# Four weight and value loads joined in pairs, a longer whole part of the seventh w2, and a copy shared by two engines

## The chip, the cores and the metric

The kernel runs on one core of a Trainium2 chip. The metric is the device time of one execution in microseconds (us); the time before is the median of three runs, 179.95 us (179.82 to 180.35).

A core has five engines with an instruction queue each, which work in order: TensorE (PE), VectorE (DVE), ScalarE (ACT), GpSimd (POOL) and SyncE (SP). Data moves between the chip's memory and the on-chip memory by transfers that an engine issues and sixteen DMA engines carry out. In this kernel POOL issues the loads and SP the stores of the result.

## The reference

Attention over 8 batches of 8 heads with 576 rows of 64 values, then a mixture of 8 experts over 32 slots. Heads 0 to 3 see the last 32 positions ("plain"), heads 4 to 7 every fourth of the last 128 ("dilated"). Cut to what matters:

```python
scores = np.where(masks, (q @ k.T) / 8, -1e9)
attn = softmax(scores, axis=-1) @ v                 # 8 batches, 8 heads, 576 x 64
x = attn.transpose(0, 2, 1, 3).reshape(4608, 512)
logits = x @ phi                                    # phi: 512 x 32
slot_input = softmax(logits, axis=0).T @ x          # 32 slots x 512, four slots an expert
for e in range(8):                                  # w1: 512 x 1024, w2: 1024 x 512, each expert its own
    slot_out[4*e : 4*e+4] = np.maximum(slot_input[4*e : 4*e+4] @ w1[e], 0) @ w2[e]
out = softmax(logits, axis=1) @ slot_out            # 4608 x 512, float32
```

## The kernel before

Inputs are float32 in memory and are converted to float16 by the loads themselves; the output is float32.

**Homes.** On-chip memory for loads is four buffers (`home0`, `home2`, `home4`, `home6`) of 2 x 8192 float16 values in each of 128 partitions, so one half (`homes[b]`) for each of 8 batches. When batch b is done with, its half takes expert b's weights: w1 in its values 0 to 4095, w2 in 4096 to 8191.

**Loads.** All of them stand in POOL's queue in the order in which the code calls them. `load_batch(b)` (L180) issues for one batch: q and k of the plain heads, v (for batches from 2 on all eight heads in one load, L238), `vt` (the last 64 rows of v, L240), and q and k of the dilated heads, which batches 2/3, 4/5 and 6/7 share in one load for two batches (L207). The eight batches come first. The weights follow: w1 and w2 of experts 0/1 and 2/3 as pairs (`load_w1(e, 2)` L286, `load_both_w2` L293), issued in the loop over units after units 6 and 14; after unit 22 the pair w1(4,5) and the single w2(4); after unit 26 the single w1(6); behind the loop w1(7), w2(5), w2(6) and w2(7) (L732 to L735). A load waits until its place is free, that is until the engines have read the batch there, and until the load eight places ahead of it has landed: eight semaphores go round.

**The last two w2.** Each expert's w2 lies as 8 chunks of 512 columns. The seventh one, w2(6), comes in three loads: chunks 0 to HALF-1 whole (HALF = 4, L309), then the other chunks' columns 0 to 255 (side 0) and 256 to 511 (side 1) by `load_half` (L300). The eighth, w2(7), comes by sides, each in two pieces of 6 and 2 chunks (L325). The order is: w2(6) whole part, w2(6) side 0, w2(7) side 0, w2(6) side 1, w2(7) side 1. So side 0 of the slots' output can be finished while side 1 is still being loaded.

**Compute.** The loop runs over 32 units (a batch and a pair of heads). Behind it comes a part whose order on PE, DVE and ACT is written out by hand (from L737). In it the experts run in pairs `pr`: `expert_in(pr)` (L794) multiplies the slots with both w1, `expert_turn(pr)` (L809) transposes the result (DVE copies it, L818), `expert_out(e)` (L823) multiplies with w2 and adds into one accumulator `sop`. PE's order (L837 to L848) is

```python
    expert_in(0)
    expert_in(1)
    for pr in range(4):
        expert_turn(pr)
        if pr < 2:
            expert_in(pr + 2)
        if pr == 1:
            front_sums(B - 1, ring.tile([128, 11, N_SLOTS], FP32, name="sums", tag="ring"))
        if pr < 3:
            expert_out(2 * pr)
            expert_out(2 * pr + 1)
    expert_out(6, chs=range(HALF))
```

Then, for each side (L892), come the rest of `expert_out(6)`, `expert_out(7)`, a copy of that side of `sop` to float16 (`so`, L895: side 0 by ACT, side 1 by DVE), and for the first three of nine output tiles of 512 rows four finishing matmuls each (`f`, L865), whose results ACT and DVE scale in turn into `ot` (L869, L871), and a store by SP (L881). The other six tiles are finished over the whole width at the end (L887).

In the texts below out(e) is `expert_out(e)`, in(pr) is `expert_in(pr)`, and w1(6,7) is one load for two experts.

Of the kernel before, what the change touches and what calls it, by code (L numbers as in the profile page):

```python
# [14 lines left out]
H = 8  # L15
S = 576
D = 64
# [6 lines left out]
E_EXP = 8  # L24
# [6 lines left out]
RP, NP = 6, 96  # L31
RD = 24
# [5 lines left out]
NV = 2  # L38
SIDES = ((0, DMODEL // 2), (DMODEL // 2, DMODEL))
PIECES = ((0, 6), (6, 8))  # L40
HALF = 4
FIRST_TILES = 3
PAIRED = (2, 4, 6)
TOGETHER = ((3,), (4, 5), (6,), (7,), (8,))
# [3 lines left out]
def kernel(  # L48
# [10 lines left out]
    nc = tc.nc  # L59
# [13 lines left out]
    first = {}  # L73
    for n, (nm, ten, by) in enumerate((("qp", q, nc.sync), ("kp", k, nc.scalar))):
        first[nm] = stage[0:NP, 768 * n : 768 * n + 768].rearrange("p (g x) -> p g x", g=2)
        by.dma_start(
            out=first[nm],
            in_=ten[0, 0:2].rearrange("h s d -> (h s) d").rearrange("(g p r) d -> p g (r d)", g=2, r=RP),
# [8 lines left out]
    for n in (1, 2, 4, 8, 16, 32, 64, 128):  # L87
        m = min(n, QW - n)
        nc.vector.tensor_scalar(
            out=count[:, n : n + m], in0=count[:, 0:m], scalar1=float(n), scalar2=None, op0=ALU.add  # L90
# [28 lines left out]
    vp = [kept([128, NKB + 1, 4, D + 1], f"vp{i}") for i in range(NV)]  # L119
    vd = [kept([128, 16, D + 1], f"vd{i}") for i in range(2)]  # L120
# [18 lines left out]
    twos = [big.tile([128, 2, 8192], FP16, name=f"home{i}", tag=f"home{i}") for i in (0, 2, 4)]  # L139
# [40 lines left out]
    def load_batch(b):  # L180
        if b == 6:
            twos.append(big.tile([128, 2, 8192], FP16, name="home6", tag="home6"))
            homes.extend(twos[3][:, i] for i in range(2))
        t = homes[b]
        parts = raws.setdefault(b, {})
        at = 0

        def load_v(nm, h0, n_h, r0, dst):
            n_p = dst.shape[0]
            dst = dst.rearrange("p (h x) -> p h x", h=n_h)  # L190
            nc.gpsimd.dma_start(  # L191
                out=dst,
                in_=v[b, h0 : h0 + n_h, r0 : r0 + 4 * n_p, :].rearrange(
                    "h (p r) d -> p h (r d)", r=4
                ),
            )
            parts[nm] = dst.rearrange("p h (r d) -> p h r d", r=4)

        for nm, ten, hs, rows in (
            ("qp", q, 0, RP), ("kp", k, 0, RP), ("qd", q, 4, RD), ("kd", k, 4, RD),  # L200
        ):
            g = 4 * S // (NP * rows)
            n = g * rows * D
            if nm in ("qd", "kd") and b & 6 in PAIRED:
                if b % 2 == 0:
                    both = twos[b // 2][0:NP, :, at : at + n]
                    nc.gpsimd.dma_start(  # L207
                        out=both,
                        in_=ten[b : b + 2, hs : hs + 4].rearrange("e h s d -> e (h s) d").rearrange(
                            "e (p r) d -> p e (r d)", r=rows  # L210
                        ),
                    )
                    for i in range(2):
                        raws.setdefault(b + i, {})[nm] = both[:, i : i + 1]
                at += n
                continue
            parts[nm] = t[0:NP, at : at + n].rearrange("p (g x) -> p g x", g=g)
            at += n
            src = ten[b, hs : hs + 4].rearrange("h s d -> (h s) d").rearrange(
                "(g p r) d -> p g (r d)", g=g, r=rows  # L220
            )
            if b == 0 and nm in first:
                t0 = side_by_side(nm[0], 0)
                nc.vector.tensor_copy(
                    out=t0.rearrange("p r (h d) -> p r h d", h=2),
                    in_=first[nm].rearrange("p h (r d) -> p r h d", d=D),
                )
                nc.gpsimd.dma_start(out=parts[nm][:, 2:4], in_=src[:, 2:4])
            else:
                nc.gpsimd.dma_start(out=parts[nm], in_=src)  # L230
            if nm == "kp":
                if b == 0:
                    head_v = t[:, 6144:7168].rearrange("p (h x) -> p h x", h=4)
                    parts["vp"] = head_v.rearrange("p h (r d) -> p h r d", r=4)
                elif b < 2:
                    load_v("vp", 0, 4, 0, t[:, 6144:7168])
                else:
                    load_v("v", 0, 8, 0, t[:, 6144:8192])  # L238
                    parts["vp"], parts["vd"] = parts["v"][:, 0:4], parts["v"][:, 4:8]
                load_v("vt", 0, 8, 512, t[96:112, 0:2048])  # L240
        if b < 2:
            load_v("vd", 4, 4, 0, t[:, 7168:8192])

    def cast_first_v():
# [35 lines left out]
    def load_w1(e, n=1):  # L280
        for i in range(e, e + n):
            w_tiles[i] = [
                homes[i][:, 0:4096].rearrange("p (c f) -> p c f", c=4),
                homes[i][:, 4096:8192].rearrange("p (c f) -> p c f", c=8),
            ]
        nc.gpsimd.dma_start(  # L286
            out=homes[e][:, 0:4096] if n == 1 else twos[e // 2][:, :, 0:4096],
            in_=moe_w1[e].rearrange("(p c) f -> p (c f)", p=128) if n == 1
            else moe_w1[e : e + 2].rearrange("e (p c) f -> p e (c f)", p=128),
        )  # L290

    def load_both_w2(e):
        nc.gpsimd.dma_start(  # L293
            out=twos[e // 2][:, :, 4096:8192],
            in_=moe_w2[e : e + 2].rearrange("e (p c) f -> p e (c f)", p=128),
        )
# [8 lines left out]
    def load_w2(e):  # L305
        w2t = w_tiles[e][1]
        w2_from = moe_w2[e].rearrange("(p c) f -> p c f", p=128)
        if e == E_EXP - 2:
            nc.gpsimd.dma_start(  # L309
                out=w2t[:, 0:HALF].rearrange("p c f -> p (c f)"),  # L310
                in_=w2_from[:, 0:HALF].rearrange("p c f -> p (c f)"),
            )
            load_half(e, 0)
            return
        if e < E_EXP - 2:
            nc.gpsimd.dma_start(
                out=w2t.rearrange("p c f -> p (c f)"), in_=w2_from.rearrange("p c f -> p (c f)")
            )
            return
        w2t = w_tiles[e][1] = w2t.rearrange("p c f -> p (c f)").rearrange("p (s c f) -> p s c f", s=2, c=8)  # L320
        for n, (d0, d1) in enumerate(SIDES):
            if n == 1:
                load_half(e - 1, 1)
            for c0, c1 in PIECES:
                nc.gpsimd.dma_start(out=w2t[:, n, c0:c1], in_=w2_from[:, c0:c1, d0:d1])  # L325
# [350 lines left out]
    for u in range(NU - 2):  # L676
        b, ph = divmod(u, 4)
        if ph == 0:
            st = scores(u + 1)
            softmax_parts(u + 1, st)  # L680
            if u:
                x_transposes(u - 1)
            values(u)
        elif ph == 1:
            st = scores(u + 1)
            if b + 1 < B:
                regroup(4 * b + 4)
            if b:
                front_logits(b - 1)
            if b + 1 < B:  # L690
                transposes(4 * b + 4)
            values(u)
            x_transposes(u - 1)
            softmax_parts(u + 1, st)
        elif ph == 2:
            st = scores(u + 1)
            values(u)
            if b + 1 < B:
                regroup(4 * b + 6)
            softmax_parts(u + 1, st)  # L700
            if b + 1 < B:
                dilated_transposes(b + 1, "k")
                dilated_transposes(b + 1, "q")
            if b:
                front_rows(b - 1)
            x_transposes(u - 1)
            if u == 2:
                nc.vector.tensor_copy(out=vd[1][:, 0, 0:1], in_=xs[0][:, 0, 2 * D : 2 * D + 1])
        else:
            st = scores(u + 1)  # L710
            if b:
                front_slots(b - 1)
            values(u)
            softmax_parts(u + 1, st)
            if b + 1 < B:
                select_v(b + 1)
                transposes(4 * b + 6)
            x_transposes(u - 1)
            if b + 1 < B:
                spread_v(b + 1)  # L720
        if u in (6, 14):
            load_w1(u // 4 - 1, 2)
            load_both_w2(u // 4 - 1)
        if u == 22:
            load_w1(4, 2)
            load_w2(4)
        if u == 26:
            load_w1(6)
        if 26 <= u:
            nc.gpsimd.memset(hTp[u - 26], 0.0)  # L730

    load_w1(E_EXP - 1)  # L732
    load_w2(E_EXP - 3)
    load_w2(E_EXP - 2)
    load_w2(E_EXP - 1)  # L735

# [25 lines left out]
    for c in range(2):  # L762
# [14 lines left out]
        out=siT,  # L777
# [114 lines left out]
    for n, (d0, d1) in enumerate(SIDES):  # L892
        expert_out(E_EXP - 2, n, range(HALF, 8))
        expert_out(E_EXP - 1, n)
        (nc.scalar.copy if n == 0 else nc.vector.tensor_copy)(out=so[:, d0:d1], in_=sop[:, d0:d1])  # L895
        for i in range(FIRST_TILES):
            finish_half(i, n)
    for tiles in TOGETHER:
# [35 lines left out]
```

## Time and profile before

| what | value |
|---|---|
| median of three runs | 179.95 us (179.82 to 180.35) |
| the profiled execution, its time | 180.08 us |
| its span, first to last instruction | 177.9 us |
| PE, ACT, DVE, POOL busy | 82%, 70%, 68%, 24% of the span |
| moved by DMA | 41.28 MB in 27094 packets |
| read from and written to the chip's memory | 61.93 MB and 9.44 MB, 401 GB/s over the span |
| first store of the result issued at | 152.15 us |
| last store of the result issued | in a row of five that starts at 160.25 us and lasts 6.92 us |

Times inside the execution count from the span's start. The profile's page divides the span into 40 equal slices; each digit of a row is the busy share of a slice in tenths, the row DMA is the mean over the sixteen DMA engines, and the row GB/s says what they moved. The bytes of a converting load are counted as float16, half of what is read. A stretch's line gives its length, then for each engine the busy us and the number of instructions, then the granted clock of TensorE as a share of the full one, the DMA share and GB/s. A timeline's line gives start, duration, engine, line, operation, result and operands, and in brackets how long the engine had been idle and what ended that. The DMA share can be above 1 where packets of one engine overlap.

### The profile page before, as it was taken

The numbers are of one execution on the slowest core, as the hardware profiler recorded it, in microseconds if no ns is written. First come the engines' busy times: TensorE is split into PE (matmuls) and PEld (weight loads), VectorE is DVE, ScalarE is ACT, GpSimd is POOL, SyncE is SP. The second block draws the span as 40 slices with busy tenths as digits, with TensorE's granted clock in tenths as the row PEclk, the third lists the DMA queues.
The fourth block names the chain that finished last, engine by engine and source line by source line (L and its number), as shares of the span: only waits on it lengthen the run. The fifth ranks groups of instructions, "written<-read, shape, count | busy, mean of one in ns | idle before, by whom it ended". The sixth has DMA issues, their size and how long they took to land.

```text
span 177.9 us, 5105 instructions
## 1 busy us (share of the span) xinstructions
PE 145.3 (82%) x2137; PEld 99.4 (56%) x2137; DVE 120.3 (68%) x337; ACT 124.0 (70%) x233; POOL 43.2 (24%) x68
## 2 busy tenths in 40 slices
PE   6589889899999999999999999977899833897200
PEld 2367576687676676776677676755763311453000
DVE  7959896987988888898798898587120100689400
ACT  2588899999998998998998999952304100699300
POOL 7756443334333441001000500700011100000000
PEclk9987999999999999999999999996558985569955
DMA  5999999999999999999999999999999999999996
GB/s 162 243 198 207 199 205 212 199 200 204 212 200 201 202 213 199 217 223 214 214 219 215 215 217 217 214 219 214 214 221 214 208 197 194 252 382 423 431 424 267
DMA packets 27094, 41.28 MB, mean 232 GB/s; under 512 B 1344, under 2 KB 22848, under 8 KB 24512
## 3 DMA queue, kind: packets, MB, share of 16 engines
q0 software_dynamic: 22080, 30.41, 96.1%
q1 hardware_dynamic: 4784, 10.26, 14.9%
q10 hardware_dynamic: 208, 0.29, 0.6%
q8 instruction: 16, 0.26, 0.5%
q14 instruction: 6, 0.05, 0.1%
HBM read 61.93 MB, written 9.44 MB: 401 GB/s over the span
## 4 chain that ended last, share of the span: by engine, by line
DMA 47%; PE 31%; ACT 6%; DVE 5%; issue 2%; POOL 1%; DVEq 0%; ACTq 0%; POOLq 0%
DMA home<-in_moe_w_dram 37%; DMA home<-in_k_dram 9%; PE o L496 6%; PE f L865 4%; PE s L391 3%; PE rgx L516 3%; PE sel L270 2%; PE sel L259 2%; ACT kTd L364 2%; PE rgq L351 2%; ACT pd L424 2%; PE rgk L351 2%; PE l L534 1%; DVE ot L871 1%; ACT ot L869 1%
## 5 line engine op out<-in xcount | busy, mean ns | idle before, releaser
L501 DVE TENSOR_TENSOR x<-o,rc 128x640 f16<-128x640 f32 x32 | 26.6, 831 | 0.2
L417 ACT ACTIVATE pr<-s 128x960 f16<-128x960 f32 (+1 forms) x32 | 25.2, 795 | 0.0
L424 ACT ACTIVATE pd<-s 128x640 f16<-128x640 f32 x32 | 22.3, 719 | 1.1 <-PE s L400 1.0
L871 DVE TENSOR_SCALAR ot<-f,rrow 128x256 f32<-128x256 f32 (+1 forms) x24 | 13.2, 613 | 7.8 <-PE f L865 7.8
L433 DVE TENSOR_TENSOR Pp<-pr,fixed 128x1280 f16<-128x1280 f16 (+1 forms) x32 | 15.4, 520 | 0.0
L496 PE MATMUL o<-vd,P 128*128 128x65 f16 x256 | 15.1, 197 | 0.2 <-DVE x L501 0.2
L191 POOL DMA_DIRECT2D home<-in_v_dram x17 | 12.0, 709 | 13.1 <-DMA home<-in_k_dram 6.1
L869 ACT ACTIVATE ot<-f,rrow 128x256 f32<-128x256 f32 (+1 forms) x24 | 12.7, 583 | 2.6 <-PE f L865 2.2
L496 PE MATMUL o<-vp,Pp 128*128 128x65 f16 x288 | 13.7, 197 | 1.0 <-DVE x L501 1.0
L516 PE MATMUL rgx<-fixed,x 128*128 128x128 f16 x155 | 14.0, 222 | 0.6 <-ACT qTd L364 0.4
L865 PE MATMUL f<-so,ET 128*128 128x256 f16 (+1 forms) x48 | 12.3, 411 | 2.2 <-ACT ot L869 1.1
L286 POOL DMA_DIRECT2D home<-in_moe_w_dram x5 | 3.2, 637 | 41.5 <-PE sel L270 38.0
L352 ACT COPY qT<-rgq 128x576 f16<-128x576 f16 x16 | 10.3, 645 | 4.0 <-PE rgq L351 3.9
L391 PE MATMUL s<-qT,kTp 64*128 64x160 f16 (+1 forms) x160 | 10.6, 224 | 2.9 <-ACT pd L424 1.9
L534 PE MATMUL l<-xT,phi 128*128 128x288 f16 x64 | 11.6, 307 | 1.6 <-DVE xT L526 1.6
L496 PEld LDWEIGHTS <-P 128*128 128x128 f16 x288 | 11.8, 99 | 1.8 <-DVE xT L526 0.2
L522 ACT COPY xT<-rgx 128x512 f16<-128x512 f16 x16 | 9.7, 605 | 4.3 <-PE rgx L516 4.3
L496 PEld LDWEIGHTS <-Pp 128*128 128x128 f16 x288 | 11.1, 99 | 2.4 <-DVE x L501 1.2
L363 PEld LDWEIGHTS <-home 96*128 96x128 f16 x192 | 10.5, 100 | 3.1 <-DMA home<-in_k_dram 1.0
L391 PE MATMUL s<-qTd,kTd 64*128 64x144 f16 x128 | 12.1, 230 | 0.0
L443 DVE TENSOR_TENSOR P<-pd,fixed 128x1024 f16<-128x1024 f16 x16 | 10.9, 681 | 1.8 <-ACT pd L424 1.8
L516 PEld LDWEIGHTS <-x 128*128 128x128 f16 x160 | 10.2, 98 | 3.1 <-DVE x L501 1.6
(136 smaller groups left out, 318.3 us busy)
## 6 DMA issues: line engine op xcount, KB each, us to landing
home<-in_moe_w_dram POOLq DMA_DIRECT2D x5, 2048.0 KB, 38.9
home<-in_moe_w_dram POOLq DMA_DIRECT2D x4, 1024.0 KB, 33.9
out_dram<-ot SPq DMA_DIRECT2D x4, 1024.0 KB, 8.5
home<-in_v_dram POOLq DMA_DIRECT2D x6, 512.0 KB, 14.3
home<-in_q_dram POOLq DMA_DIRECT2D x9, 288.0 KB, 12.9
home<-in_k_dram POOLq DMA_DIRECT2D x9, 288.0 KB, 13.4
out_dram<-ot SPq DMA_DIRECT2D x4, 512.0 KB, 3.6
out_dram<-ot SPq DMA_DIRECT2D x1, 2048.0 KB, 6.8
```

What stands on the lines that cost most here:

```text
L191: nc.gpsimd.dma_start(out=dst, in_=v[b, h0 : h0 + n_h, r0 : r0 + 4 * n_p, :].rearrange("h (p r) d -> p h (r d)", r=4),)
L391: nc.tensor.matmul(st[:, g, at : at + n], kT[64 * g : 64 * g + 64, k0 : k0 + 128], qT[64 * g : 64 * g + 64, q0 : q0 + n], start=True, stop ...
L417: nc.scalar.activation(out=(pr[:, :, 0 : 3 * QW], pr[:, :, 3 * QW :])[part], in_=st[:, :, 0 : (480, 224)[part]], func=AF.Exp, scale=SCALE,)
L424: nc.scalar.activation(out=pr[:, part].rearrange("p c e t -> p e c t"), in_=st[:, :, 0 : 2 * DW].rearrange("p e (c t) -> p e c t", c=2), f ...
L433: nc.vector.tensor_tensor(out=Pp[:, :, b0 : b0 + nb, 0:w], in0=pr[:, :, b0 * QW : b0 * QW + nb * w].rearrange("p h (t c) -> p h t c", c=w) ...
L496: nc.tensor.matmul(ot[:, h, blk], lhs, rhs, start=(n == 0), stop=(n == len(mms) - 1), skip_group_check=True)
L501: nc.vector.tensor_tensor(out=xs[b][:, :, 2 * D * hp : 2 * D * hp + 2 * D].rearrange("p t (h d) -> p h t d", h=2), in0=ot[:, :, :, 0:D], i ...
L516: nc.tensor.transpose(rg[:, 128 * blk : 128 * blk + 128], x[:, blk, hl : hl + 128], ident)
L534: nc.tensor.matmul(lp, phi4[:, kc].rearrange("p a s -> p (a s)"), xT[:, kc, 288 * c : 288 * c + 288], start=(kc == 0), stop=(kc == 3), ski ...
L865: nc.tensor.matmul(fp, ET[:, c0 : c0 + 127 * nj + 1 : nj], so[:, d0:d1], start=True, stop=True)
L869: nc.scalar.activation(out=ot[:, j], in_=fp, func=AF.Copy, scale=scale)
L871: nc.vector.tensor_scalar(out=ot[:, j], in0=fp, scalar1=scale, scalar2=None, op0=ALU.mult)
```

## The change

- v of batches 4 and 5 comes in one load, and v of batches 6 and 7 too. Batches 2 and 3 keep their own. For this q, k and v of the paired batches get other places in the home, and in the paired batches v is issued ahead of the dilated q and k as before.
- w2(4) and w2(5) come as a pair after unit 22, where w2(4) alone was issued. w1(6) and w1(7) come as a pair behind the loop; w1(6) after unit 26 is gone. So w2(5) goes ahead of w1(6) and w1(7) in POOL's queue.
- HALF is 6: six chunks of w2(6) come whole, and two by sides. `expert_out(6)` ahead of the sides takes six chunks.
- The copy of each side of `sop` is split by columns, 128 by ACT and 128 by DVE.

The diff, cut to its core:

```diff
-HALF = 4
+HALF = 6
...
         def load_v(nm, h0, n_h, r0, dst):
...
+                in_=v.rearrange("b h s d -> (b h) s d")[
+                    H * b + h0 : H * b + h0 + n_h, r0 : r0 + 4 * n_p, :
+                ].rearrange("h (p r) d -> p h (r d)", r=4),
...
+        at = (10240 + 2 * n * (b % 2)) if paired else 0
...
+        if paired:
+            if b < 4:
+                load_v("v", 0, H, 0, t[:, 6144:8192] if b == 2 else t[:, 0:2048])
+            elif b % 2 == 0:
+                load_v("v", 0, 2 * H, 0, flat[:, 6144:10240])
+            load_v("vt", 0, H, 512, t[96:112, 2048:4096])
+            parts["vp"], parts["vd"] = parts["v"][:, 0:4], parts["v"][:, 4:8]
...
         if u == 22:
             load_w1(4, 2)
-            load_w2(4)
-        if u == 26:
-            load_w1(6)
+            load_both_w2(4)
...
-    load_w1(E_EXP - 1)
-    load_w2(E_EXP - 3)
+    load_w1(E_EXP - 2, 2)
     load_w2(E_EXP - 2)
     load_w2(E_EXP - 1)
...
-        (nc.scalar.copy if n == 0 else nc.vector.tensor_copy)(out=so[:, d0:d1], in_=sop[:, d0:d1])
+        mid = (d0 + d1) // 2
+        nc.scalar.copy(out=so[:, d0:mid], in_=sop[:, d0:mid])
+        nc.vector.tensor_copy(out=so[:, mid:d1], in_=sop[:, mid:d1])
```

More of the change, by code (lines that the diff above doesn't have):

```diff
@@ L185, in load_batch @@
         parts = raws.setdefault(b, {})
-        at = 0
+        paired = b & 6 in PAIRED
+        flat = twos[b // 2].rearrange("p e x -> p (e x)")
+        n = S * 4 * D // NP
         def load_v(nm, h0, n_h, r0, dst):
@@ L192, in load_v @@
                 out=dst,
-                in_=v[b, h0 : h0 + n_h, r0 : r0 + 4 * n_p, :].rearrange(
-                    "h (p r) d -> p h (r d)", r=4
-                ),
-            )
[L197 to L217, printed above, removed]
+                in_=v.rearrange("b h s d -> (b h) s d")[
+                    H * b + h0 : H * b + h0 + n_h, r0 : r0 + 4 * n_p, :
+                ].rearrange("h (p r) d -> p h (r d)", r=4),
+            )
+            got = dst.rearrange("p h (r d) -> p h r d", r=4)
+            if n_h <= H:
+                parts[nm] = got
+            else:
+                for i in range(2):
+                    raws.setdefault(b + i, {})[nm] = got[:, H * i : H * i + H]
+        at = (10240 + 2 * n * (b % 2)) if paired else 0
+        for nm, ten in (("qp", q), ("kp", k)):
+            home = flat if paired else t
+            parts[nm] = home[0:NP, at : at + n].rearrange("p (g x) -> p g x", g=4)
             at += n
[L219 to L222, printed above, removed]
+            src = ten[b, 0:4].rearrange("h s d -> (h s) d").rearrange("(g p r) d -> p g (r d)", g=4, r=RP)
+            if b == 0:
                 t0 = side_by_side(nm[0], 0)
@@ L230, in load_batch @@
                 nc.gpsimd.dma_start(out=parts[nm], in_=src)
[L231 to L241, printed above, removed]
+        if b == 0:
+            head_v = t[:, 6144:7168].rearrange("p (h x) -> p h x", h=4)
+            parts["vp"] = head_v.rearrange("p h (r d) -> p h r d", r=4)
+        elif not paired:
+            load_v("vp", 0, 4, 0, t[:, 6144:7168])
+        if paired:
[5 more added lines that the diff above has]
+            parts["vp"], parts["vd"] = parts["v"][:, 0:4], parts["v"][:, 4:8]
+        else:
+            load_v("vt", 0, H, 512, t[96:112, 0:2048])
+        for i, (nm, ten) in enumerate((("qd", q), ("kd", k))):
+            if not paired:
+                at = 3072 + n * i
+                parts[nm] = t[0:NP, at : at + n][:, None, :]
+                nc.gpsimd.dma_start(
+                    out=t[0:NP, at : at + n],
+                    in_=ten[b, 4:8].rearrange("h s d -> (h s) d").rearrange("(p r) d -> p (r d)", r=RD),
+                )
+            elif b % 2 == 0:
+                both = flat[0:NP, 2 * n * i : 2 * n * i + 2 * n].rearrange("p (e x) -> p e x", e=2)
+                nc.gpsimd.dma_start(
+                    out=both,
+                    in_=ten[b : b + 2, 4:8].rearrange("e h s d -> e (h s) d").rearrange(
+                        "e (p r) d -> p e (r d)", r=RD
+                    ),
+                )
+                for j in range(2):
+                    raws.setdefault(b + j, {})[nm] = both[:, j : j + 1]
+        if not paired:
             load_v("vd", 4, 4, 0, t[:, 7168:8192])
```

## The prediction

> **What bounds the kernel now.** I read the page's slices first, then the chain of waits, then stretches of the last 55 us, then PE's timeline there.
>
> ```profile
> DMA  5999999999999999999999999999999999999996
> GB/s 162 243 198 207 199 205 212 199 200 204 212 200 201 202 213 199 217 223 214 214 219 215 215 217 217 214 219 214 214 221 214 208 197 194 252 382 423 431 424 267
> ```
>
> The DMA row is full from the second slice to the last but one. Loads convert f32 to f16, so 215 GB/s counted at the f16 side is about 430 GB/s read, the rate at which the f32 outputs leave (423 to 431). The core is bound by its 16 DMA engines nearly throughout; the attention work of PE, ACT and DVE lies beside it. The next answer gives, for each stretch, its length, busy us of each engine, the granted clock, the DMA share and GB/s.
>
> ```profile
> 74.49:124.00 49.51, 45.38 (x797) 33.78 (x795) 41.26 (x104) 42.42 (x82) 7.22 (x12) 0.97 1.03 216
> 124.00:144.00 20.00, 17.07 (x204) 10.13 (x204) 3.19 (x15) 3.87 (x9) 3.00 (x4) 0.73 1.03 213
> 144.00:151.00 7.00, 2.67 (x29) 0.96 (x22) 0.26 (x2) 0.37 (x1) 0.00 (x0) 0.59 1.40 196
> 151.00:153.50 2.50, 2.50 (x12) 1.57 (x11) 1.93 (x5) 2.14 (x6) 0.00 (x0) 0.50 0.95 150
> 153.50:162.00 8.50, 7.33 (x38) 3.72 (x38) 6.96 (x14) 6.64 (x15) 0.00 (x0) 0.68 1.08 386
> 162.00:176.00 14.00, 3.30 (x11) 1.13 (x10) 4.77 (x8) 3.93 (x7) 0.00 (x0) 0.75 1.01 428
> ```
>
> One stretch is not full: 150 GB/s at 151.0 to 153.5. The trace marks a load's completion once per DMA engine, and the marks of the very last load spread from 151.25 to 154.11: seven engines are done by 152.1, nine only after 153.1. So the end has two bounds. The slowest engine: loads done at 154.11, plus the outputs (3.15 MB at 386 GB/s, 8.15 us, and 6.29 MB at 428, 14.7 us) gives 176.96; the last output lands at 177.00. The fast engines wait for outputs: the first is issued at 152.15, they have written it at 154.10 and the last one at 176.59, 24.44 us after that first issue. The slack between the two bounds is only 0.4 us. What the change does to **the last load** and to **the first output's issue** decides.
>
> The first output hangs on side 0 of the slots, as PE's timeline shows (start, duration, what, and in brackets idle time and what ended it).
>
> ```profile
> 137.85 0.40 PE L799 MATMUL h<-home,siT 128*32 128x512 f16 x2
> 138.76 1.08 PE L799 MATMUL h<-home,siT 128*32 128x512 f16 x14 [0.50 <-DMA home<-in_moe_w_dram]
> 139.77 0.43 PE L584 MATMUL sums<-quarter,ET 128*128 128x1 f16 x8
> 140.13 1.05 PE L828 MATMUL sop<-home,hTp 128*32 128x512 f16 x16
> 141.10 0.41 PE L813 MATMUL tp<-fixed,hs 128*128 128x128 f16 x4
> 141.79 0.62 PE L828 MATMUL sop<-home,hTp 128*32 128x512 f16 x8 [0.27 <-DVE hTp L818]
> 143.63 0.62 PE L828 MATMUL sop<-home,hTp 128*32 128x512 f16 x8 [1.22 <-DMA home<-in_moe_w_dram]
> 144.18 0.41 PE L813 MATMUL tp<-fixed,hs 128*128 128x128 f16 x4
> 146.14 0.62 PE L828 MATMUL sop<-home,hTp 128*32 128x512 f16 x4 [1.55 <-DMA home<-in_moe_w_dram]
> 147.46 0.41 PE L828 MATMUL sop<-home,hTp 128*32 128x256 f16 x4 [0.71 <-DMA home<-in_moe_w_dram]
> 149.41 1.07 PE L828 MATMUL sop<-home,hTp 128*32 128x256 f16 x8 [1.54 <-DMA home<-in_moe_w_dram]
> ```
>
> The starts behind a DMA date the landings: seventh w1 pair's second half 138.7, sixth w2 143.6, then 2.51 us for 512 KB whole, 1.32 for 256 KB in half rows, 1.95 for 384 KB; the last 128 KB (0.68) lands at 150.05.
>
> **Four loads fewer.** Pairs of w1(6,7), w2(4,5), v(4,5) and v(6,7) replace eight loads by four; bytes and run lengths stay. What does one load cost beside its bytes? On the engine that marks first, half-row loads take 0.675 us for 128 KB, 1.33 for 256, 2.00 for 384: a straight line with 0.01 us at zero. Two single 1 MB loads take 4.85 and 4.87, a 2 MB pair 9.71: 0.01. The short v tails of 64 KB take 0.35 to 0.46 where the bytes are worth 0.33: up to 0.13, part of it their row shape. A loss is excluded on the queue, since POOL issues 15 to 39 us before landing and six to eight loads wait at any time. Bounds 0 to 0.13 each; I take 0.025, nearest to the rows of the same sizes: 4 x 0.025 = **-0.1 us**. The 0.5 to 0.9 us of POOL per issue lie under that queue.
>
> [...]
>
> The v pairs put 512 KB (2.7 us) ahead of the rest of batches 4 and 6. Batch 4's kd lands at 50.9 and its transposes begin at 64: covered by 10 us.
>
> **Six chunks whole.** 256 KB change from half rows (1.32) to whole rows (2.51 / 2 = 1.25): **-0.07**. Loads thus end at 154.11 - 0.17 = 153.94. But side 0 now waits for more: 768 KB whole (3.77) + 0.68 + 1.95 + 0.68 = 7.08 us behind the sixth w2, instead of 2.51 + 1.32 + 1.95 + 0.68 = 6.46. With the -0.1, its last piece lands at 150.05 + 0.62 - 0.1 = **150.57**.
>
> **The moved w1.** w2(5) goes ahead of w1(7), and w1(6,7) has one completion: both land where w2(5) did, near 143.5 instead of 133.9 and 138.7. PE executes in order, and behind expert_in(3) are queued the sums, out(2) to out(5), two turns and out(6): all that ran from 137.85 to 146.7 now starts at 143.5. Its length, wave by wave (four matmuls side by side): at full clock in(3) 0.9, sums 0.46, out(2,3) 0.86, turn with DVE's copy 0.78, out(4,5) 0.86, turn 0.78, out(6) six chunks 0.43, side 0's last ten matmuls and drain 0.58: 5.65 us. At half clock a wave takes 0.427 instead of 0.216 (rows at 132 to 134), and the same list gives 10.0.
>
> Which clock? In stretches of 2 us the granted clock is 0.50 until 135.0, 1.00 until 145.2, 0.50 until 158.9: it rose after a full 3.4 us of matmuls, and fell after 3.4 us with PE 45% busy. PE would now idle from 137.9 to 143.5, 5.6 us, so I take half clock at the start and a rise at the end of the first full window, 148.6 if the windows fall as here. Then 5.1 of 10.0 are done by 148.6 and the rest takes 4.9 x 0.565 = 2.8: side 0 is complete at **151.4**, against 150.49. PE, not the load (150.57 + 0.3), is late next. By the window's phase the rise lies between 146.6 and 150.0: 150.9 (the load's bound) to 152.0.
>
> [...]
>
> **The slots' copy.** ScalarE took 0.37 for 256 columns and 0.60 for 512, so 0.26 for 128; VectorE 0.42 for 256 and 0.21 for 64, so 0.28. The longer of two beside each other: 0.28 against 0.37, -0.09 on side 0. Side 1's 0.42 - 0.28 lies under outputs already queued: 0. The risk that the second engine is busy is nil on side 0 (both idle since 144.9). At full clock the first two finishing matmuls end some 0.2 earlier (second starts 0.11 instead of 0.21 later, drain 0.1 shorter): -0.2.
>
> **Sum.** First output: 152.15 + 0.91 - 0.09 - 0.2 = 152.77, so 24.44 later the engines end at 177.21; the slowest engine's own bound is 177.00 - 0.17 = 176.83. The later counts: +0.2 us. The profiled execution took 180.08 (span 177.93), 0.13 above the median of 179.95. So 179.95 + 0.2 = **180.1** (180.15 cut to tenths). Own range, by 0.1 either way in the loads and by a rise at 146.6 to 149: 179.7 to 180.5.
>
> **Rivals.**
> Slower, one mechanism: PE's clock comes back late. Each us of rise beyond 148.6 costs 0.43. At 150.0, side 0 is complete at 152.0 and the end is 180.7; if the clock stays at half, 153.5, the 0.2 is gone too, and the end is 182.4. It decides from a rise at 149.5. For it: 62% and 83% busy windows at 148.6 to 155.5 did not raise it, and the new stretch has gaps at the two turns. Against: without waits for DMA these gaps are some 0.3 us. Chance 0.25.
> Faster: the loads are cheaper by the upper bound (4 x 0.13, 0.5 us) and the clock rises early, so that the load bounds side 0 at 150.2 + 0.3: first output 152.15 + 0.0 - 0.29 = 151.9, and the slowest engine ends at 177.00 - 0.6: 179.35. For it: the short v tails. Against: the sizes that are really paired show 0.01. Chance 0.18.
> [...] The equal spacing of queued loads leaves it 0.02. That the change does less than it says is excluded: in the built programs POOL issues 56 loads instead of 60, and PE's order changes only where out(6) takes six chunks.
>
> **Numbers.** Forecast 0.55, slower rival 0.25, faster 0.2. 0.3%, 0.54 us, is about what a measurement of this kernel can tell from no change. The range takes in the faster rival and the slower one up to a rise 2.4 us late (0.43 x 2.4 = 1.0): 179.3 to 181.2.
>
> **What would show it.** Right: PE idle from about 138 until the pair lands near 143.5, a granted clock of 0.5 there and 1.0 before 149; side 0's copy near 151.4; the first output at 152.8; the 150 GB/s stretch emptier and later; the last load at 153.9. Wrong: a pair of w1 that lands before 142 (loads cost more than I took), a clock that did not fall in PE's idle time, or outputs that do not keep their 24.44 us.

## The result, and the profile after

The changed kernel takes 180.48 us (median of 22 runs), the kernel before 179.84 (22 runs beside them). The ratio is 1.0041, 95% interval 1.0023 to 1.0059: slower by 0.2 to 0.6%. More telling than the median is the spread. The kernel before lies between 179.71 and 180.36. The changed one begins at the same place, 179.79, and reaches 181.55: fifteen of its 22 runs lie between 179.79 and 180.95, the other seven between 181.42 and 181.55.

The profiled execution is the fastest of them, 179.79 us with a span of 177.9. So it shows the change at its best, and the long runs have to be read from the experiments. The rows of its page that answer to those of before:

```profile
DMA  5999999999999999999999999999999999999996
GB/s 149 247 199 206 199 202 214 200 199 200 208 211 198 199 209 207 221 215 219 212 217 219 214 217 217 214 215 221 214 212 223 211 199 194 231 385 422 433 425 282
```

The DMA row is as full as before. The same stretches (length, busy us of each engine, granted clock, DMA share, GB/s) show the change at the end:

```profile
144.00:151.00 7.00, 6.28 (x80) 2.46 (x69) 0.72 (x5) 0.69 (x2) 0.00 (x0) 0.77 1.32 194
151.00:153.50 2.50, 1.93 (x15) 1.23 (x15) 1.82 (x5) 1.82 (x6) 0.00 (x0) 1.00 0.85 116
153.50:162.00 8.50, 6.96 (x40) 3.67 (x40) 7.83 (x17) 7.57 (x17) 0.00 (x0) 1.00 1.08 385
```

PE is busy for 6.28 us from 144 to 151, where it had 2.67. The stretch that was not full moves 116 GB/s instead of 150: the DMA engines that are done with their loads wait longer, since the first store is issued at 152.55 instead of 152.15. PE's timeline says why it is busy so late:

```profile
139.82 0.41 PE L822 MATMUL tp<-fixed,hs 128*128 128x128 f16 x4
143.58 1.72 PE L808 MATMUL h<-home,siT 128*32 128x512 f16 x16 [3.34 <-DMA home<-in_moe_w_dram]
145.24 0.42 PE L596 MATMUL sums<-quarter,ET 128*128 128x1 f16 x8
145.59 1.84 PE L837 MATMUL sop<-home,hTp 128*32 128x512 f16 x16
147.36 0.41 PE L822 MATMUL tp<-fixed,hs 128*128 128x128 f16 x4
148.04 1.05 PE L837 MATMUL sop<-home,hTp 128*32 128x512 f16 x16 [0.27 <-DVE hTp L827]
149.02 0.41 PE L822 MATMUL tp<-fixed,hs 128*128 128x128 f16 x4
149.70 1.18 PE L837 MATMUL sop<-home,hTp 128*32 128x512 f16 x16 [0.27 <-DVE hTp L827]
151.55 0.71 PE L874 MATMUL f<-so,ET 128*128 128x256 f16 x5 [0.68 <-DVE so L906]
```

The second line is in(3): it waited until w1(6,7) landed. Sixteen of `sop`'s matmuls take 1.84 us at 145.6 and 1.05 at 148.0: the granted clock was 0.50 from 143.8 to 147.2 and 1.00 behind it. Here the list ends with side 0's last load (150.55), so the late w1 costs nothing in this run. The copies and the first store, in the timelines of ACT, DVE and SP:

```profile
150.91 0.27 ACT L905 CAST so<-sop 128x128 f16<-128x128 f32 x1 [4.91 <-PE sop L837]
```
```profile
151.21 0.29 DVE L906 CAST so<-sop 128x128 f16<-128x128 f32 x1 [1.48 <-ACT so L905]
```
```profile
152.55 5.87 SPq L890 DMA_DIRECT2D out_dram<-ot  x8
```

The two half copies do not run beside each other: DVE's waits for ACT's and starts 0.03 us after its end.

### The profile page after: what moved, and what is told of

Its sections match the earlier page's. It is cut to its first block, busy times and chain, and to the rows that moved or that the text cites. A ratio compares the mean times of both kernels' runs of the same rounds, so it can differ in the third digit from the quotient of the medians.

```text
span 177.9 us, 5100 instructions
## 1 busy us (share of the span) xinstructions
PE 145.7 (82%) x2135; PEld 99.9 (56%) x2135; DVE 120.4 (68%) x338; ACT 123.5 (69%) x234; POOL 40.4 (23%) x64
## 4 chain that ended last, share of the span: by engine, by line
PE 49%; DVE 13%; ACT 12%; DMA 11%; issue 7%; POOL 0%; DVEq 0%; ACTq 0%; POOLq 0%
DMA home<-in_moe_w_dram 11%; PE o L508 11%; PE s L403 5%; PE rgx L528 4%; PE sel L282 4%; PE sel L271 4%; ACT ot L878 4%; ACT kTd L376 3%; DVE P L455 3%; PE warm L480 3%; PE rgq L363 3%; PE rgk L363 2%; ACT pd L436 2%; PE l L546 2%; PE u L609 2%
## 5 line engine op out<-in xcount | busy, mean ns | idle before, releaser
L878 ACT ACTIVATE ot<-f,rrow 128x256 f32<-128x256 f32 (+1 forms) x24 | 11.9, 604 | 1.7 <-DMA home<-in_moe_w_dram 0.7
L874 PE MATMUL f<-so,ET 128*128 128x256 f16 (+1 forms) x48 | 10.7, 324 | 2.5 <-DVE so L906 1.4
L193 POOL DMA_DIRECT2D home<-in_v_dram x15 | 10.8, 717 | 8.4 <-DMA home<-in_q_dram 3.9
```

What stands on the lines that cost most here:

```text
L193: nc.gpsimd.dma_start(out=dst, in_=v.rearrange("b h s d -> (b h) s d")[H * b + h0 : H * b + h0 + n_h, r0 : r0 + 4 * n_p, :].rearrange("h ( ...
L878: nc.scalar.activation(out=ot[:, j], in_=fp, func=AF.Copy, scale=scale)
```

## The experiments

Two theories stood. The first: **PE's list behind the late w1** ends last, at a clock that differs from run to run, and the copy and the later load of side 0 add to it. The second: the **joined loads** themselves, or the six whole chunks, cost the time. Eleven kernels were run beside the kernel before.

| kernel | runs | median, lowest to highest, us | ratio to before (interval) | first store issued, us |
|---|---|---|---|---|
| the change | 22 | 180.48, 179.79 to 181.55 | 1.0041 (1.0023 to 1.0059) | 152.55 |
| move_only | 12 | 180.40, 179.76 to 181.49 | 1.0026 (1.0003 to 1.0048) | 154.07 |
| half6_only | 12 | 180.31, 179.94 to 180.70 | 1.0016 (1.0004 to 1.0028) | 153.24 |
| split_only | 12 | 179.98, 179.81 to 180.11 | 0.9989 (0.9974 to 1.0003) | 152.41 |
| v_only | 12 | 180.02, 179.70 to 180.41 | 1.0006 (0.9993 to 1.0018) | 152.15 |
| one_copy | 12 | 180.07, 179.54 to 181.07 | 1.0004 (0.9986 to 1.0023) | 153.90 |
| half4 | 12 | 180.02, 179.74 to 181.38 | 1.0008 (0.9992 to 1.0025) | 152.38 |
| w1_first | 5 | 182.72, 181.96 to 183.07 | 1.0144 (1.0121 to 1.0167) | 155.40 |
| w1_ahead | 12 | 180.48, 180.15 to 180.70 | 1.0019 (1.0006 to 1.0032) | 152.93 |
| warmed | 6 | 181.41, 181.16 to 182.05 | 1.0079 (1.0058 to 1.0101) | 152.62 |
| moved_warm | 13 | 180.01, 179.80 to 183.69 | 0.9997 (0.9982 to 1.0012) | 156.31 (in its run of 183.58) |
| mended | 11 | 179.70, 179.56 to 179.91 | 0.9988 (0.9979 to 0.9997) | 151.90 |

The first store is that of one profiled execution, which may lie anywhere in its kernel's spread (179.79 for the change, 181.22 for `move_only`, 181.07 for `one_copy`). Each ratio is to runs of the kernel before beside that kernel (medians 179.84 to 179.89), and is not the quotient of the two medians. The ratio of `moved_warm` leaves out its two runs above 183.

**One part alone.** `move_only` is the kernel before with the order of the weights as changed:

```diff
             load_w1(4, 2)
-            load_w2(4)
-        if u == 26:
-            load_w1(6)
+            load_both_w2(4)
...
-    load_w1(E_EXP - 1)
-    load_w2(E_EXP - 3)
+    load_w1(E_EXP - 2, 2)
```

> The kernel before with the joined w2(4,5) and w1(6,7) in the order of the change, nothing else (two loads fewer). Theory (PE's list behind the late w1, clock by the run): w1(6,7) lands near 143.5, runs spread from 179.7 to some 181.0, median 180.0 to 180.2. Rival (the moved load is covered): 179.8 with the small spread of before.

It has the spread of the whole change, up to 181.49, and a median of 180.40, above the 180.2 expected. (Two of the 35 runs of the kernel before beside it reached 180.96 and 180.98, none reached 181.) Its profile is of a run of 181.22. PE's timeline in it:

```profile
143.75 1.90 PE L796 MATMUL h<-home,siT 128*32 128x512 f16 x16 [5.17 <-DMA home<-in_moe_w_dram]
145.58 0.42 PE L584 MATMUL sums<-quarter,ET 128*128 128x1 f16 x8
145.94 1.90 PE L825 MATMUL sop<-home,hTp 128*32 128x512 f16 x16
147.77 0.61 PE L810 MATMUL tp<-fixed,hs 128*128 128x128 f16 x4
148.65 1.90 PE L825 MATMUL sop<-home,hTp 128*32 128x512 f16 x16 [0.27 <-DVE hTp L815]
150.48 0.61 PE L810 MATMUL tp<-fixed,hs 128*128 128x128 f16 x4
151.36 1.23 PE L825 MATMUL sop<-home,hTp 128*32 128x512 f16 x16 [0.27 <-DVE hTp L815]
153.08 1.11 PE L862 MATMUL f<-so,ET 128*128 128x256 f16 x7 [0.48 <-ACT so L892]
```

Every entry from in(3) at 143.75 to the turn at 150.48 has the length of half clock: 1.90 us for sixteen matmuls that take 1.09 (in(2), at 135.63) and 1.05 (out(2) and out(3), at 140.13) in the kernel before at a granted 1.00. (The short sums take 0.42 here and 0.43 there.) Side 0's last load has landed at 150.18, and PE reaches it at the end of the line at 151.36. In the traces of the kernel before and of the change, the times at which the granted clock changes lie whole multiples of 3.41 us apart (before, 121.34, 134.99, 145.23 and 158.88: four, three and four of them); such a stretch of 3.41 us is called a window here. The two windows ahead of the rise, cut at their borders:

```profile
145.61:149.03 3.42, 3.15 (x36) 1.27 (x36) 0.47 (x3) 0.60 (x1) 0.00 (x0) 0.50 1.45 196
149.03:152.44 3.41, 3.14 (x36) 1.14 (x28) 0.26 (x2) 0.00 (x0) 0.00 (x0) 0.50 1.24 168
```

PE was busy for 92% of the first and the clock stayed at half; it was busy for 92% of the second and the clock rose at 152.44. `one_copy` shows the same: a window of 94% at half clock left it there, and one of 90% raised it at 151.94. In the profile of the change and of `half4` the window in question was 100% busy, and the clock rose at its end (147.2 and 147.7). But the busy share doesn't decide it: in the kernel before, a window that was 100% busy at half clock did not raise it either.

```profile
124.75:128.16 3.41, 3.41 (x22) 2.88 (x21) 0.28 (x2) 1.48 (x5) 0.22 (x1) 0.50 1.04 216
128.16:131.58 3.42, 2.84 (x48) 2.48 (x44) 1.13 (x4) 0.00 (x0) 0.78 (x1) 0.50 1.06 223
```

What tells these windows apart was not found.

`half6_only` is the kernel before with one line changed, `split_only` with the two copies:

```diff
-HALF = 4
+HALF = 6
```

> The kernel before with HALF = 6 (six chunks of w2(6) whole), nothing else. Theory (side 0's last load lands 0.6 us later, all else covered): first output 152.75 instead of 152.15, end 24.44 later at 177.2, against 177.0: 0.1 to 0.3 us slower in every run, no spread. Rival (the whole rows, 0.07 us cheaper, count): 0.05 to 0.1 us faster.

The loss is there, but larger than expected and with a spread of 0.8 us: six runs lie between 179.94 and 180.14, six between 180.49 and 180.70. In its profile, of a run of 180.56, side 0's last load lands at 151.14 on the slowest DMA engine, and not near 150.65, and the first store follows 2.1 us later, as in the kernel before. So in that run a DMA engine that was some 0.5 us later than expected shows in the time. That this makes the upper six runs is likely, but only one of them was profiled.

```diff
-        (nc.scalar.copy if n == 0 else nc.vector.tensor_copy)(out=so[:, d0:d1], in_=sop[:, d0:d1])
+        mid = (d0 + d1) // 2
+        nc.scalar.copy(out=so[:, d0:mid], in_=sop[:, d0:mid])
+        nc.vector.tensor_copy(out=so[:, mid:d1], in_=sop[:, mid:d1])
```

> The kernel before with the copy split between ACT and DVE, nothing else. Theory (halves one behind the other): the first output comes 0.22 us later, 152.37, and 24.44 later is 176.81, still short of the slowest engine's 177.0: 0 to 0.1 us slower than before. Rival (halves side by side): no change or 0.1 faster. A loss of over 0.3 us would say that the stores' start counts for more than the two bounds tell.

DVE's copy starts 0.03 us after ACT's ends here too, and the first store comes at 152.41, where 152.37 was expected. The time does not show it (interval 0.9974 to 1.0003): 0.26 us is less than the slack of 0.4 us between the two bounds.

`v_only` is the change with all but the joined v undone.

> The kernel before with v of batches 4 and 5, and 6 and 7, in one load each (two loads fewer), nothing else. Theory (0.01 to 0.05 us for a load that is queued behind others): 0 to 0.1 us faster. Rival (a fixed cost in line that the equal spacing hides): 0.3 us faster or more; or a loss, where the larger load comes too late for batch 4.

No difference that can be told, and the last load lands at 154.01 instead of 154.11. The rival, 0.3 us or more by a large fixed cost in line, is excluded: the lower end of the interval, 0.9993, is 0.13 us faster.

**One part undone.** `one_copy` is the change with the copy of before, `half4` the change with HALF = 4.

> The changed kernel with the copy of before (side 0 by ACT alone, side 1 by DVE alone). Theory (the two half copies run one behind the other, 0.27 + 0.03 + 0.29 = 0.59 us against 0.37): the first output comes 0.2 us earlier whatever PE's clock does, median 180.2 to 180.3, the slow runs near 181.3 remain. Rival (the halves run side by side and save 0.09): 0.1 us slower than the change.

> The changed kernel with HALF = 4 as before: side 0's last load lands near 149.95 instead of 150.55. Theory (PE's list ends last in the slow runs): those runs stay at 181.2 to 181.5 and only runs bound by the load gain, down to about 179.6; median 180.2 to 180.4. Rival (the later data of side 0 makes the loss): median back at 179.9, no run over 180.5.

Both have a median near that of before and keep runs over 181, at 181.03 and 181.07 (two of 12) and 181.38 (one of 12). So those come without the split copy and without the six chunks. Both medians are lower than expected, by 0.1 and 0.2 us. `one_copy` is faster than the change at both ends, by 0.25 us at the lowest and 0.48 at the highest. With 12 runs spread over 1.5 us, how the 0.6 us divides between the parts stays rough.

**Taking the wait away.** `w1_first` issues w1(6,7) ahead of the joined w2(4,5):

```diff
             load_w1(4, 2)
-            load_both_w2(4)
...
     load_w1(E_EXP - 2, 2)
+    load_both_w2(4)
     load_w2(E_EXP - 2)
```

> The changed kernel, but the joined w1(6,7) is issued ahead of the joined w2(4,5); loads, bytes and the rest as in the change. Theory (PE's list behind the late w1 is what ends last, at a clock that depends on the run): w1(6,7) lands near 134, so behind 143.5 us PE has only out(4,5), a turn and out(6), 3.5 us even at half clock, and side 0 is bound by its last load (150.55); first output near 152.8, time 180.0 to 180.2, ratio to before about 1.001, and the spread over runs shrinks from 1.8 us to some 0.5. Rival (the joined loads themselves, or the six whole chunks, cost the time): the time stays near 180.5 with the same spread.

The expectation failed by 2.5 us, and PE's timeline says where:

```profile
137.31 0.61 PE L808 MATMUL h<-home,siT 128*32 128x512 f16 x2
143.61 1.89 PE L808 MATMUL h<-home,siT 128*32 128x512 f16 x14 [5.69 <-DMA home<-in_moe_w_dram]
144.87 2.33 PE L837 MATMUL sop<-home,hTp 128*32 128x512 f16 x16
```

These are in(2) and out(0), out(1): two matmuls with w1(4) ran, those with w1(5) waited until 143.6, when w2(4,5) landed. In the built program in(2) waits for that load, though it does not read it. The joined load writes two stretches of the home, w2(4) and w2(5), and w1(5) lies between them. With w2(4) and w2(5) as two single loads (`w1_ahead`, below) in(2) starts at 136.17 without a wait. That the wait comes from the outer bounds of what the joined load writes is a guess; no run tested it further. In the change the same wait stands, and costs nothing there, since w2(4,5) lands at 133.9. So this kernel lengthened PE's list by in(2), out(0), out(1) and a turn, and became 2.2 us slower than the change: the first theory, by accident, with a longer list.

`w1_ahead` does it properly, with w2(4) and w2(5) as single loads behind w1(6,7):

```diff
     load_w1(E_EXP - 2, 2)
+    load_w2(E_EXP - 4)
+    load_w2(E_EXP - 3)
     load_w2(E_EXP - 2)
```

> The changed kernel with the joined w1(6,7) ahead of w2(4) and w2(5), which come as two single loads, so that in(2) waits for no w2 (in w1_first it waited for the joined w2(4,5), by the order of the built program). Theory (PE's list behind the late w1): in(2) and in(3) run before 140, behind 143.5 PE has out(5), a turn and out(6) alone; side 0 is bound by its load, first output 152.6 to 152.9 in every run, end 24.44 us later, time 179.9 to 180.3, no run over 180.6. Rival (six whole chunks and the copy make the spread): runs up to 181.5 stay.

No run is over 181 any more: the spread shrinks from 1.76 to 0.55 us. PE's timeline waits for loads again, as before:

```profile
143.55 0.62 PE L838 MATMUL sop<-home,hTp 128*32 128x512 f16 x8 [0.72 <-DMA home<-in_moe_w_dram]
147.27 0.96 PE L838 MATMUL sop<-home,hTp 128*32 128x512 f16 x8 [2.76 <-DMA home<-in_moe_w_dram]
149.90 1.15 PE L838 MATMUL sop<-home,hTp 128*32 128x256 f16 x8 [1.67 <-DMA home<-in_moe_w_dram]
151.73 1.01 PE L875 MATMUL f<-so,ET 128*128 128x256 f16 x4 [0.68 <-DVE so L907]
```

The median, 180.48, is 0.2 above what was expected. What is left is the later load (150.61) and the copies one behind the other, at half clock: the first store at 152.93. That no run reaches 179.8 any more is likely to have the same cause: PE idles for 2.76 and 1.67 us in the last two waits above, and the granted clock is 0.5 at side 0 (from 148.1 to 154.9 in this profile), while it is 1.0 there in the change's shortest run. This rests on one profile of each.

**Keeping the clock up.** `warmed` puts idle matmuls into PE's wait; `moved_warm` takes twelve of them from the kernel's start instead:

```diff
         expert_turn(pr)
+        if pr == 1:
+            wt = ps_t.tile([128, 8, 4, N_SLOTS], FP16, name="wt", tag="tp").rearrange("p a b s -> p (a b s)").bitcast(FP32)
+            warm(14, heat, wt)
         if pr < 2:
```

> The changed kernel with 14 idle matmuls (512 columns, into a spare PSUM tile) put into PE's order between the second turn and in(3), where PE waits for w1(6,7). They add work and take none away. Theory (clock): PE is at full clock when the pair lands at 143.5, its list of 5.7 us is done by 149.3, side 0 is bound by its load (150.55); first output near 152.55, median 179.8 to 180.0, no run over 180.5. Rival (the loads or the copy cost the time, not the clock): median stays near 180.5 or goes up, with runs at 181.5.

The clock did what was meant: in(3) takes 1.09 us and the first store is issued at 152.62. Yet every run is over 181. The page's rows of DMA show why, with the queue that brings instructions:

```profile
DMA  5999999999999999999999999999999999999993
...
q8 instruction: 17, 0.28, 0.6%
```

The last slice is down to 3, and the instruction queue moved 17 blocks of 16 KB where every other kernel here moved 16. In the trace the seventeenth starts at 162.1 us and takes 0.96 us, on one DMA engine, amid the stores. Fifteen engines mark the last store's end at 176.9 to 177.1, the sixteenth at 178.5. The only edit is the 14 idle matmuls, which add 28 instructions, so they must have brought the seventeenth block. The cost was of the experiment's own making, and it was done again without adding instructions:

```diff
-    warm(12, heat)
...
+            warm(12, heat, wt)
```

> The changed kernel with the twelve idle matmuls of the kernel's start moved into PE's wait for w1(6,7); the number of instructions is that of the change, so no further block of instructions has to be fetched during the stores, as it was in warmed at 162 us (one DMA engine then ended 1.5 us behind the others). The first batch runs at a lower clock, which the wait for w1(6,7) hides. Theory (clock, and in warmed the fetch): first output near 152.6, time 179.8 to 180.2, no run over 180.6. Rival (idle matmuls themselves cost, or the clock isn't what spreads the runs): 180.5 and more, as in the change.

Eleven of 13 runs lie between 179.80 and 180.29. With seven of 22 over 181.4 as in the change, 11 in a row without one would come 1 or 2 times in 100 ((15/22)^11); nothing in the loads was changed. With the half clock in the profiles of `move_only` and `one_copy`, and with no run over 181 in `w1_ahead` and `mended`, where PE's list no longer hangs on the late w1, this says that PE's clock after the wait makes the long runs. None of the eleven runs was profiled. The other two, 183.58 and 183.69, are of another kind: in the profile of the first, groups of six transposes take 0.66 us until 39 us and 0.43 behind it, where the kernel before is at 0.41 from 16.5 us on. The work behind the loop begins late: in(0) starts at 139.4 us, against 131.9 in the kernel before and 134.5 in the change. Why two of 13 runs went that way is open.

**A version from these.** `mended` keeps the joined v and the joined w1(6,7) in the order of `w1_ahead`, with HALF = 4 and the copies of before:

```diff
-            load_both_w2(4)
...
     load_w1(E_EXP - 2, 2)
+    load_w2(E_EXP - 4)
+    load_w2(E_EXP - 3)
...
-HALF = 6
+HALF = 4
...
-        nc.scalar.copy(out=so[:, d0:mid], in_=sop[:, d0:mid])
-        nc.vector.tensor_copy(out=so[:, mid:d1], in_=sop[:, mid:d1])
+        (nc.scalar.copy if n == 0 else nc.vector.tensor_copy)(out=so[:, d0:d1], in_=sop[:, d0:d1])
```

> The joined v and the joined w1(6,7), issued ahead of the single w2(4) and w2(5); HALF = 4 and the copies of before: three loads fewer. Theory (nothing of it reaches PE's list or side 0): the last load 0.05 to 0.1 us earlier, 179.75 to 179.85, spread as before. Rival (joined loads lose by themselves): 180.2 and more.

It is the fastest kernel of the study, by 0.03 to 0.21% over before, and its spread is the smallest but one. These joined loads lose nothing by themselves; the last load lands at 153.91, 0.2 us earlier than before, where 0.05 to 0.1 was expected. What the gain comes from was not taken apart further. Its stores begin at 151.90, those of `move_only` at 154.07:

```profile
151.90 6.43 SPq L891 DMA_DIRECT2D out_dram<-ot  x8
```
```profile
154.07 5.82 SPq L878 DMA_DIRECT2D out_dram<-ot  x8
```

## Why the prediction was right in the main, and which steps of it failed

**What bounds the end** held in nearly every profile. From the first store's issue to the last mark of the last store it is 24.45 us in the change, 24.44 in `one_copy`, `move_only` and `moved_warm`, 24.43 in `w1_first`, 24.53 in `half4`, 24.56 in `w1_ahead` and `half6_only`. (The forecast's 24.44 counts to the first of these marks; counted so, the other kernels give 24.27 to 24.39.) In the kernel before (24.85), `split_only` (24.64), `mended` (24.92) and `v_only` (24.81) the last marks lie 0.26 to 0.53 us apart, and the slowest engine ends last; in `warmed` (25.88) it is the one behind the seventeenth block. Elsewhere the end is read off the first store's issue, to a tenth of a us.

**The loads** came out as worked in the change's profile: the last one at 153.95 (forecast 153.94), side 0's last at 150.55 (150.57), w1(6,7) at 143.54 (near 143.5). Two single 1 MB loads and one joined load take the same time: on the engine that marks first, w1(7) and w2(5) took 4.87 us each before, and the joined w1(6,7) 9.72 in the change. `v_only` agrees, with a ratio of 1.0006 for two loads fewer.

**The copy** is the step that failed outright. It was put at 0.28 against 0.37, a gain of 0.09 us. It takes 0.27 + 0.03 + 0.29 = 0.59 us, a loss of 0.22. The sizes of the halves were right (0.26 and 0.28 were forecast); that they run beside each other was not. The two halves lie in one accumulator, and the built program has DVE wait for ACT: 0.03 us lie between the end of ACT's copy and the start of DVE's, in the change and in `split_only`. That both write `so` is not the reason as far as the trace shows: ACT (from 151.86) and DVE (from 151.97) write their rows of one `ot` side by side, each from an accumulator of its own. The accumulator, one for both copies and one each there, differs between the two cases; whether it is the reason no run tested. The order of the built program shows that wait; the prediction had used that order for the loads and for PE alone.

**The clock** was right as a mechanism (half when the pair lands, a rise some windows later, PE's list late next) and mis-sized as a number. The forecast took a rise at 148.6 as the likeliest and 150.0 as the latest by the window's phase. The profiles show 147.2 (the change), 147.7 (`half4`), 151.9 (`one_copy`) and 152.4 (`move_only`). In the latter two the first whole window takes in one of the 0.27 us gaps at the turns, and the clock rose a window later; that the gaps are the reason is not shown, since the next window had such gaps too and raised it. The step behind the number is the premise that a full window raises the clock. The forecast read its row of before as a full 3.4 us of matmuls ahead of the rise at 135.0, but PE was busy there for 3.06 us of 3.41, and the 100% window at 124.75 had left the clock at half.

So the outcome is not one time but two groups: fifteen runs of the change up to 180.95, with a median of 180.18, and seven near 181.5. The median of all, 180.48, lies in the upper half of the first group, and the seven lie above the forecast's range of 179.3 to 181.2. The seven are the slower rival, given 0.25 (by the profiles of `move_only` and `one_copy`; no long run of the change itself was profiled), near its price: at 0.43 us for each us beyond 148.6, a rise at 151.9 comes to 181.5, and `one_copy`, with a single copy, took 181.07 there. What spreads the fifteen over 1.2 us was not found; three of the 22 runs of the kernel before also lie apart, at 180.26 to 180.36.

**The sum.** In the profiled run the first store came at 152.55, 0.2 us earlier than the forecast's 152.77. That is luck: side 0's copy began at 150.91, some 0.5 us earlier than the 151.4 that was worked out, since the clock rose early, and the copies took 0.31 us longer. With the copy alone put right, the forecast's own working gives a first store at 153.08 and an end at 177.52, 0.5 us later than before. Measured: 0.64 between the medians. The range holds the median; the case within 0.3%, taken as the likeliest, was not the one that came (0.41%). The faster rival, given 0.18, and 0.2 with the 0.02 for a fixed cost of each load, did not come: no run shows such a cost, and `v_only`, with two loads fewer, came to a ratio of 1.0006 (0.9993 to 1.0018).

**The gain at full clock** (0.2 us from the first finishing matmul to the first store) held in this run: 1.00 us from 151.55 to 152.55 at a granted 1.00, against 1.20 at 0.50 before.

## What to carry to other kernels

A load that is joined with a later one lands with the later one (w1(6) at 143.5 instead of 133.9 us here): ask first what is queued, in order, behind the instruction that waits for the earlier half, and at what clock that list will run. When the time of a kernel spreads, compare its lowest and highest runs and not only medians; the changed kernel's fastest run equalled that of before and hid everything. And splitting a copy between two engines gains only if the halves run beside each other; here they ran one behind the other, in 0.59 us where one engine took 0.37, which the built order of instructions tells without a run.

## What the runs showed of the hardware

- Blocks of instructions are fetched by the same DMA engines that carry the data: 16 KB each, 0.89 to 0.98 us in the traces of before and the change. Such a block leaves one of the sixteen marks of a load about 1.1 us behind the others: in the change the marks of a load lie 0.45 us apart at 18.5 us, as the first block starts (18.55 us), and 1.6 us at 21.1 us. The marks of later loads stay behind: in the kernel before they lie 0.6 us apart at 13.9 us, ahead of the first block (16.3 us), and 2.85 us apart at 154.1 us, after the sixteenth. In `warmed`, where a block starts during the stores (162.1 us), one engine ended at 178.5 us, the others by 177.1.
- The busy share of PE in a 3.41 us window does not tell what the clock does next. At half clock, windows of 80% (`split_only`, up to 153.84), 86% (`mended`, up to 153.65) and 87% (`v_only`, up to 154.90) raised it, and windows of 94% (`one_copy`) and 100% (the kernel before, 124.75 to 128.16, and `split_only`, 126.53 to 129.95) did not.
- A load that writes two separate stretches made an instruction wait that reads only between them (`w1_first`, 5.7 us).
